# Batch 2 of a fused attention and feed-forward kernel: q before k, halved units, earlier loads

## The chip, the cores and the metric

The kernel runs on one core of a Trainium2 chip. The metric is the device time of one execution in microseconds (us). A core has TensorE for matrix products (PE in the profile, PEld for its weight loads), VectorE (DVE), ScalarE (ACT) and GpSimd (POOL) for elementwise work, and SyncE (SP), which here issues nearly all DMA transfers. Each engine works through its own queue in order, and semaphores tie the queues together.

## The reference

Eight batches of eight heads, 576 tokens and 64 features go through a linear attention whose features carry a cosine and a sine of the position. The result, 4608 tokens of 512 features, goes through a two-layer feed-forward network with a leaky ReLU.

```python
q_p = phi(q, cos_w, sin_w)      # concat(relu(q) * cos, relu(q) * sin)
k_p = phi(k, cos_w, sin_w)
kv = np.einsum('bhsf,bhsd->bhfd', k_p, v)
z = np.sum(k_p, axis=2)
num = np.einsum('bhsf,bhfd->bhsd', q_p, kv)
den = np.einsum('bhsf,bhf->bhs', q_p, z)[..., None] + 1e-06
x = num / den                   # then tokens in rows, all heads side by side
h = x @ w_in                    # 512 -> 2048
g = np.maximum(0.01 * h, h)
out = g @ w_out                 # 2048 -> 512
```

## The kernel before, in words

**Tiling.** Each batch gives a group of 512 tokens in four slices j of 128. The remaining 64 tokens of all batches make up a ninth group. Products run in float16 with float32 sums in PSUM.

**The steps of a batch.** `load_main` (L88) and `load_kvtail` (L98) bring q, k and v into staging buffers; `load_k` and `load_v` also bring the 64 tail tokens. A staging buffer is shared by tensors in turn, so a load waits until the tensor before it has been read. `q_part` and `k_part` (L337, L269) apply relu and the cosine (part 0) or sine (part 1), on VectorE or ScalarE. This is what the change's name calls rotating. `v_main` and `v_tail` (L278, L281) cast v. `q_transpose_dma` (L345) turns a slice of q with a DMA from SyncE's queue. `kv_all` (L309) makes kv on TensorE: for each half of the heads sixteen matmuls on the main tokens, and then two on the tail. ScalarE copies it out. `num` (L376) multiplies a slice of q with kv and calls `divide` (L390), three VectorE steps (den, rden, xs). Its sums lie in the PSUM pool "n", which has one buffer. kv_all and the f1 pair m = 2, 3 use that pool as well. `x_transpose` (L442) turns xs back on TensorE into the pool "o", and ScalarE copies it into xT.

**Feed-forward.** `f1_pair` (L746) makes one tile m of 128 hidden features of group 1: four matmuls of 512 tokens (L496), and after every second m an Lrelu on ScalarE into g. Later groups use a scheme of seven products of half-size blocks instead of eight. `w1_sums`, `w2_sums`, `x_sums` and `g_sums` make the sums of blocks that it needs, on VectorE. `w2_sums(i, s)` (L526) makes step s for half i of the second weight. The second layer of group 1 already uses that scheme (`f2_stream(1)`, output name ps_o, L883). Its PSUM banks are opened by `open_banks` over the pools "h", "o" and "n" of the stage before.

**What sets the order.** Up to L706 the order of the instructions is the order of the code. Among the last of these lines are the end of group 0's second layer (`ffn2`, `ffn2_out`), the divisions of batch 1 (`num_half`, L408), and the first two tiles m of each half of the first layer (`f1_half`). Behind that, all steps are put on one line with a position (`put`), sorted by position, ties in the order in which they were put, and issued so. On each engine the steps run in that order. The positions stand in tables written by hand: AT for each batch (kc and ks for k's cosine and sine, with the tail as fifth entry; v; kv; qc and qs; qt for the q transposes; num; xt; load), W2_AT for `w2_sums`, G1_AT for `g_sums` of group 1. ENG says for each k, v and q step which engine does it. Positions of batches 2 and 3 count from the start of the line. Four matmuls of `f1_pair` stand at each even position 2n (L1044), and a unit below is such a group of four. The first four tiles n are made ahead of the line, so there `f1_pair` issues only the Lrelus. For batch 2 all q parts are on VectorE, k is on VectorE but for two sine slices on ScalarE, and v is shared. For batch 3 the first q cosine part and the second sine part are on ScalarE.

Of the kernel before, what the change touches and what calls it, by code (L numbers as in the profile page):

```python
# [18 lines left out]
def kernel(  # L19
# [60 lines left out]
    ACT, DVE, POOL = nc.scalar, nc.vector, nc.gpsimd  # L80
# [152 lines left out]
    kv = [const.tile([P, H, NE], dt.float16, name=f"kv{b}") for b in range(B)]  # L233
# [20 lines left out]
    def sub(o, a, b):  # L254
        nc.vector.tensor_tensor(out=o, in0=a, in1=b, op=ALU.subtract)  # L255
# [62 lines left out]
    def kv_half(b, hg, where, blanks=0):  # L318
        ps = psum(where, [P, MAIN], dt.float32, "ps_kvh")
        idle(blanks, ps)  # L320
        ps = ps[:, 0 : 4 * NE]
        kv_mm(b, hg, ps)
        nc.scalar.copy(
            kv[b][:, 4 * hg : 4 * hg + 4, 0 : NE - 1],
            ps.rearrange("p (h e) -> p h e", h=4)[:, :, 0 : NE - 1],
        )
# [10 lines left out]
    def q_part(g, j, part, eng, lo=0, hi=H):  # L337
        src, c, _ = q_src(g, j)
        if lo == 0 and part == 0:
            st["qp", g, j] = qppool.tile([P, H, F], dt.float16, name="qp", tag="qp")  # L340
        qp, f = st["qp", g, j], part * D
        col = (cos_t, sin_t)[part][:, c : c + 1]
        phi_half(eng, qp[:, lo:hi, f : f + D], src[:, lo:hi], col)
# [126 lines left out]
    def ffn2(g, i, eng=DVE):  # L470
        tt, part = divmod(i, 4)
        if part == 0 and ("ps_o", g, tt) not in st:
            st["ps_o", g, tt] = psum("o", [P, DM], dt.float32, "ps_o")
        ps = st["ps_o", g, tt]
        for m in range(4 * part, 4 * part + 4):
            nc.tensor.matmul(
                ps,
                lhsT=st["g", g][:, m, tt * P : (tt + 1) * P],
                rhs=w2[:, m, :],
                start=(m == 0),  # L480
                stop=(m == NFT - 1),
            )
        if part == 3 and eng is not None:
            ffn2_out(g, tt, eng)

    def ffn2_out(g, tt, eng):
        osb = opool.tile([P, DM], dt.float32, name="osb", tag="osb")
        copy(eng, osb, st["ps_o", g, tt])
        nc.sync.dma_start(out_rows(g)[:, tt, :], osb)
# [4 lines left out]
    def f1_mm(g, m, ps, chunks=range(NKC), lo=0, hi=MAIN):  # L494
        for c in chunks:
            nc.tensor.matmul(  # L496
                ps[:, lo:hi],
                lhsT=w1[m // 4][c // 2][:, c % 2, m % 4 : 512 : 4],
                rhs=st["xT", g][:, c, lo:hi],
                start=(c == 0 and lo == 0),  # L500
                stop=(c == NKC - 1 and hi == MAIN),
            )
# [23 lines left out]
    def w2_sums(i, s):  # L526
        lo, hi = slice(4 * i, 4 * i + 4), slice(8 + 4 * i, 12 + 4 * i)
        left, right = slice(0, N2), slice(N2, DM)
        b11, b12 = w2[:, lo, left], w2[:, lo, right]
        b21, b22 = w2[:, hi, left], w2[:, hi, right]  # L530
        if s == 1:
            sub(wb[1][:, lo], b12, b11)
        elif s == 2:
            sub(wb[2][:, lo], b22, wb[1][:, lo])
        elif s == 4:
            sub(wb[4][:, lo], b21, wb[2][:, lo])
        else:
            sub(b12, b22, b12)
# [127 lines left out]
    ps = psum("n", [P, 2, DM], dt.float32, "ps_o")  # L666
# [22 lines left out]
    ps = psum("h", [P, 2, MAIN], dt.float16, "ps_x")  # L689
    for jp in range(2):  # L690
        x_transpose_half(1, jp, 0, ps[:, :, jp * 2 * P : (jp + 1) * 2 * P], False)
    nc.scalar.copy(st["xT", 1][:, 0:2, :], ps)
    kv_half(1, 1, "n")
    ffn2_out(0, 0, DVE)
    ffn2(0, 4 * 1 + 3, None)
    ffn2_out(0, 1, ACT)
    num_half(1, 0, 1, "h")
# [45 lines left out]
                [P, NH, N2], dt.float16, name="g" + nm, tag="g" + nm, bufs=bufs  # L743
            )

    def f1_pair(g, m):  # L746

        early_ = m % NH < 2
        if m % 2 == 0 and not early_:
            st["h", m // 2] = psum("hn"[m == 2], [P, 2, MAIN], dt.float32, "ps_h")  # L750
        ps = st["h", m // 2]
        if not early_:
            f1_mm(g, m, ps[:, m % 2])
        if m % 2:
            up, u = divmod(m - 1, NH)
            nc.scalar.activation(
                st["gt", g][:, up, :, u : u + 2].rearrange("p h m n -> p m h n"),
                ps.rearrange("p m (h n) -> p m h n", h=2),
                AF.Lrelu,
            )  # L760
# [265 lines left out]
    def put(pos, f, *args):  # L1026
        line.append((pos, len(line), f, args))
# [13 lines left out]
    put(-1, quarters, 1)  # L1041
    order = [m + up for m in range(0, NH, 2) for up in (0, 1, NH, NH + 1)]
    for n, m in enumerate(order):
        put(2 * n, f1_pair, 1, m)  # L1044
    put(31, open_banks)
    put(35, blank_seed)
    for g in range(2, NG):
# [16 lines left out]


    W1_AT = {3: (43.5, 53.5)}
    W2_AT = {2: (17.0,), 3: (30.0, 18.5), 4: (75.5,)}
    G1_AT = {3: (15.0, 31.0), 2: (17.5, 33.5), 1: (25.5, 39.5), 4: (63.0, 47.0)}
    G_AT = {3: (-6.5, 10.5), 2: (11.0, 11.0), 1: (19.5, 32.5), 4: (23.0, 29.5)}
    G3_AT = {3: (-3.5, 13.0), 2: (2.0, 23.0), 1: (12.5, 29.5), 4: (26.5, 51.0)}  # L1070
# [1 line left out]
    GL_AT = {3: (-15.5, 13.0), 2: (-1.5, 13.5), 1: (5.5, 16.2), 4: (17.5, 32.0)}  # L1072
    R_AT = (29.5, 30.0, 41.0, 48.0)
    ENG = {2: {'kc': (DVE, DVE, DVE, DVE, DVE), 'ks': (ACT, DVE, DVE, ACT, DVE), 'v': (ACT, DVE, ACT), 'qc': (DVE, DVE, DVE, DVE), 'qs': (DVE, DVE, DVE, DVE)}, 3: {'kc': (ACT, ACT, ACT, DVE, DVE), 'ks': (DVE, DVE, ACT, ACT, DVE), 'v': (DVE, ACT, DVE), 'qc': (ACT, DVE, DVE, ACT), 'qs': (DVE, ACT, ACT, DVE)}, 4: {'kc': (ACT, ACT, DVE, ACT, ACT), 'ks': (DVE, ACT, DVE, DVE, DVE), 'v': (DVE, DVE, ACT), 'qc': (DVE, DVE, ACT, DVE), 'qs': (DVE, DVE, DVE, ACT)}, 5: {'kc': (DVE, DVE, DVE, DVE, DVE), 'ks': (DVE, DVE, DVE, DVE, DVE), 'v': (DVE, ACT, ACT), 'qc': (ACT, ACT, DVE, ACT), 'qs': (ACT, ACT, DVE, ACT)}}
    AT = {2: {'kc': (-12.0, -0.5, 13.0, 5.5, 13.0), 'ks': (-22.5, -12.5, -17.0, -10.5, 0.0), 'v': (11.0, 11.0, 12.5), 'kv': (16.5,), 'qc': (-8.0, 2.5, 4.5, 8.0), 'qs': (0.0, 4.5, 7.5, 13.0), 'qt': (6.0, 7.0, 8.0, 14.0), 'num': (19.0, 20.5, 24.0, 26.5), 'xt': (24.4, 24.9, 26.9, 30.9), 'xs': (35.5, 50.0, 36.0, 56.0)}, 3: {'load': (20.0, 24.0, 29.0), 'kc': (37.0, 42.5, 47.0, 49.0, 50.5), 'ks': (34.0, 43.5, 58.5, 50.5, 51.0), 'v': (56.0, 57.5, 59.0), 'kv': (62.0,), 'qc': (26.0, 28.5, 31.0, 33.5), 'qs': (31.5, 29.5, 41.0, 41.0), 'qt': (32.5, 34.5, 44.0, 53.0), 'num': (69.5, 76.0, 83.0, 89.0), 'xt': (89.5, 92.5, 93.0, 100.5), 'xs': (102.5, 106.0, 104.5, 113.5)}, 4: {'load': (-75.5, -104.5, -111.5), 'kc': (-80.0, -58.0, -55.0, -70.5, -49.5), 'ks': (-72.5, -54.5, -66.0, -55.0, -54.0), 'v': (-85.0, -40.5, -44.5), 'kv': (-37.5,), 'qc': (-72.5, -67.5, -50.0, -40.5), 'qs': (-65.5, -51.0, -43.5, -39.0), 'qt': (-52.0, -39.5, -33.0, -32.0), 'num': (-34.0, -28.3, -24.6, -16.4), 'xt': (-19.0, -16.8, -12.1, -8.4), 'xs': (-0.5, 0.0, 9.5, 16.5)}, 5: {'load': (-103.5, -85.5, -75.5), 'kc': (-64.5, -75.0, -78.0, -50.0, -49.0), 'ks': (-71.0, -59.0, -72.5, -60.5, -74.0), 'v': (-60.0, -52.0, -60.5), 'kv': (-46.5,), 'qc': (-87.0, -76.0, -44.5, -48.0), 'qs': (-72.5, -75.5, -44.0, -31.5), 'qt': (-55.0, -53.0, -43.5, -23.5), 'num': (-37.0, -32.3, -22.6, -15.9), 'xt': (-25.0, -14.8, -17.6, -8.9), 'xs': (-2.0, -2.0, -1.5, 5.0)}}

    def loads(b, which):
        if which == 0:
# [11 lines left out]
        put(W1_AT[3][i], w1_sums, i, 3, 0, 4 - 2 * i)  # L1090
    for s, at_ in zip((1, 2, 4, 3), R_AT):
        put(top[ALL - 1] + at_, w1_sums, 1, s, 2, 4)
    for s, at_ in W2_AT.items():
        for i in range(2 - len(at_), 2):
            put(at_[i - 2], w2_sums, i, s)
    for s, at_ in G1_AT.items():
        for u in range(2):
            put(at_[u], g_sums, 1, s, 4 * u, 4 * u + 4)
# [6 lines left out]
    for b in range(2, NG):  # L1105
        at_, eng, s0 = AT[min(b, 5)], ENG[min(b, 5)], top[b] if b > 3 else 0
        if b < B:
            for n, pos_ in enumerate(at_.get("load", ())):
                put(s0 + pos_, loads, b, n)
            put(s0 + min(at_["kc"] + at_["ks"]) - 0.01, kp_tiles, b)  # L1110
            for j in range(J + 1):
                put(s0 + at_["kc"][j], k_part, b, j, 0, eng["kc"][j])
                put(s0 + at_["ks"][j], k_part, b, j, 1, eng["ks"][j])
            for n in range(3):
                put(s0 + at_["v"][n], v_part, b, n, eng["v"][n])
            put(s0 + at_["kv"][0], kv_all, b)
        else:
            for j in range(J):
                put(s0 - 100 + 3 * j, load_qtail, j)
        for j in range(J):  # L1120
            put(s0 + at_["qc"][j], q_part, b, j, 0, eng["qc"][j])
            put(s0 + at_["qs"][j], q_part, b, j, 1, eng["qs"][j])
            put(s0 + at_["qt"][j], q_transpose_dma, b, j)
            put(s0 + at_["num"][j], num, b, j)
            put(s0 + at_["xt"][j], x_transpose if b == 2 else x_transpose_dma, b, j)
            put(s0 + at_["xs"][j], x_sums, b, j + 1)
# [33 lines left out]
```

## Time and profile before

| what | us |
|---|---|
| median of 3 runs | 271.92 |
| the runs | 271.84, 275.43, 271.92 |
| the profiled execution, its own time | 271.19 |
| its span, first to last instruction | 269.4 |

The page of the profile gives each engine's busy time and share of the span. Timelines list instructions in order of time, runs of like ones merged: start, duration, engine, line, operation, output and inputs, count, and in brackets the idle time before it and what ended it. The view of stretches gives the length and then for PE, PEld, DVE, ACT and POOL the busy time and the count, then the granted clock of TensorE, the DMA share and GB/s. The chain of waits lists start, duration and what was running. A DMA issue is listed with its size and the time to landing.

### The profile page before, as it was taken

How to read it: one execution, taken by the hardware profiler on the slowest of the kernel's cores; microseconds unless marked ns; L12 is line 12 of the kernel's file. 1: busy time of each engine (PE TensorE's matmuls, PEld its weight loads, DVE VectorE, ACT ScalarE, POOL GpSimd, SP SyncE). 2: the span in 40 equal slices, each digit the busy share in tenths (PEclk: the TensorE clock that was granted, in tenths of full speed). 3: DMA queues.
4: the chain of work that ended last, by engine and by line, in shares of the span. 5: the costliest groups of instructions: out<-in, count | busy, mean ns of one | idle time of the engine just before them, and what ended most of it. 6: DMA issues, size and time to landing. Idle time of an engine off the chain costs nothing.

```text
span 269.4 us, 6623 instructions
## 1 busy us (share of the span) xinstructions
PE 263.5 (98%) x2670; PEld 227.0 (84%) x2670; DVE 203.8 (76%) x452; ACT 199.4 (74%) x329; POOL 13.1 (5%) x25
## 2 busy tenths in 40 slices
PE   8999999999999999999999999999999999999994
PEld 6985455665998989899999999999999899999983
DVE  5875798797967898888879778977687758545652
ACT  8757476696888896978888788878877757666720
POOL 5047001000000000000000000000000000000000
PEclk9999999999999999999999999999999999999999
DMA  6999999979999979958995899669384412200324
GB/s 226 373 392 415 393 386 373 357 170 296 274 252 313 191 195 249 354 116 285 259 254 122 271 239 247 156 202 154 62 142 155 61 41 97 80 0 2 156 41 117
DMA packets 86190, 57.05 MB, mean 212 GB/s; under 512 B 55632, under 2 KB 81232, under 8 KB 85648
## 3 DMA queue, kind: packets, MB, share of 16 engines
q1 hardware_dynamic: 85584, 55.98, 77.0%
q8 instruction: 21, 0.34, 0.6%
q10 hardware_dynamic: 448, 0.39, 0.4%
q0 software_dynamic: 128, 0.26, 0.3%
q14 instruction: 9, 0.07, 0.1%
HBM read 36.70 MB, written 9.44 MB: 171 GB/s over the span
## 4 chain that ended last, share of the span: by engine, by line
PE 76%; DVE 2%; issue 0%
PE ps_o L883 33%; PE ps_h L782 30%; PE ps_h L496 4%; PE ps_num L381 3%; PE ps_h L883 3%; PE ps_kv L290 2%; DVE gs L255 0%; PE ps_kv L299 0%; PE ps_xt L446 0%; DVE xs L397 0%; DVE w L255 0%; DVE wb L255 0%; DVE ob L252 0%; DVE qp L241 0%; DVE kpt L241 0%
## 5 line engine op out<-in xcount | busy, mean ns | idle before, releaser
L883 PEld LDWEIGHTS <-g 128*128 128x128 f16 x648 | 62.7, 98 | 7.2 <-DVE g L252 0.3
L252 DVE TENSOR_TENSOR u<-ps_h,u 128x512 f32<-128x512 f32 x52 | 35.8, 688 | 21.0 <-PE ps_h L782 19.3
L883 PE MATMUL ps_o<-w,g 128*128 128x256 f16 x352 | 51.2, 273 | 0.0
L782 PEld LDWEIGHTS <-w 128*128 128x128 f16 x416 | 44.7, 113 | 1.2
L782 PE MATMUL ps_h<-xT,w 128*128 128x256 f16 x288 | 43.3, 273 | 0.0
L809 ACT ACTIVATE g<-u 128x1024 f16<-128x1024 f32 x26 | 27.5, 1058 | 11.2 <-DVE u L252 10.9
L802 ACT COPY u<-ps_h 128x512 f32<-128x512 f32 x52 | 30.5, 586 | 7.1 <-PE ps_h L782 7.0
L795 ACT ACTIVATE g<-ps_h 128x512 f16<-128x512 f32 x52 | 31.2, 602 | 5.6 <-PE ps_h L782 5.6
L782 PEld LDWEIGHTS <-wa 128*128 128x128 f16 x312 | 33.7, 113 | 1.2
L883 PE MATMUL ps_o<-wb,g 128*128 128x256 f16 x232 | 33.5, 273 | 0.0
L782 PE MATMUL ps_h<-xw,wa 128*128 128x256 f16 x208 | 31.3, 273 | 0.0
L883 PEld LDWEIGHTS <-gs 128*128 128x128 f16 x256 | 24.9, 98 | 2.9
L901 ACT COPY ob<-ps_o 128x512 f32<-128x512 f32 (+1 forms) x32 | 18.1, 565 | 11.9 <-PE ps_o L883 10.6
L496 PE MATMUL ps_h<-xT,w 128*128 128x512 f16 (+1 forms) x104 | 24.7, 363 | 0.0
L397 DVE TENSOR_TENSOR xs<-ps_num,rden 128x512 f16<-128x512 f32 x28 | 19.4, 691 | 1.0
L883 PE MATMUL ps_o<-w,gs 128*128 128x256 f16 x120 | 17.8, 273 | 0.0
L252 DVE TENSOR_TENSOR ob<-ps_o,ob 128x512 f32<-128x512 f32 (+1 forms) x22 | 14.9, 675 | 3.8 <-ACT ob L901 1.9
L883 PE MATMUL ps_o<-wb,gs 128*128 128x256 f16 x120 | 17.5, 273 | 0.0
L792 ACT COPY ps_h<-ps_h 128x512 f32<-128x512 f32 x26 | 14.9, 572 | 2.4 <-PE ps_h L782 1.5
L255 DVE TENSOR_TENSOR gs<-g 128x1024 f16<-128x1024 f16 x16 | 11.0, 688 | 7.3 <-ACT g L809 7.2
L782 PE MATMUL ps_h<-xw,w 128*128 128x256 f16 x104 | 15.6, 273 | 0.0
L782 PE MATMUL ps_h<-xT,wa 128*128 128x256 f16 x104 | 15.6, 273 | 0.0
(116 smaller groups left out, 411.8 us busy)
## 6 DMA issues: line engine op xcount, KB each, us to landing
qst<-in_q_dram SPq DMA_DIRECT2D x7, 1024.0 KB, 6.4
out_dram<-ob SPq DMA_DIRECT2D x14, 512.0 KB, 2.8
kst<-in_k_dram SPq DMA_DIRECT2D x6, 1024.0 KB, 7.1
vst<-in_v_dram SPq DMA_DIRECT2D x6, 1024.0 KB, 7.2
w1st<-in_moe_w_in_dram SPq DMA_DIRECT2D x8, 512.0 KB, 10.5
w2st<-in_moe_w_out_dram SPq DMA_DIRECT2D x4, 1024.0 KB, 12.3
kst<-in_k_dram SPq DMA_DIRECT2D x4, 512.0 KB, 8.1
vst<-in_v_dram SPq DMA_DIRECT2D x4, 512.0 KB, 8.3
```

The costliest lines, as they stand in the source:

```text
L252: nc.vector.tensor_tensor(out=o, in0=a, in1=b, op=ALU.add)
L255: nc.vector.tensor_tensor(out=o, in0=a, in1=b, op=ALU.subtract)
L381: nc.tensor.matmul(ps[lo:hi, h // 4, (h % 4) * NE : (h % 4 + 1) * NE - 1], lhsT=qpT[:, h, lo:hi], rhs=kv[b][:, h, 0 : NE - 1],)
L397: nc.vector.tensor_tensor(out=xs, in0=ps[:, :, 0 : 4 * NE].rearrange("p a (b e) -> p a b e", e=NE)[:, :, :, 0:D], in1=rden.rearrange("p (a ...
L496: nc.tensor.matmul(ps[:, lo:hi], lhsT=w1[m // 4][c // 2][:, c % 2, m % 4 : 512 : 4], rhs=st["xT", g][:, c, lo:hi], start=(c == 0 and lo == 0),
L782: nc.tensor.matmul(bank[:, p], lhsT=w(c), rhs=st["xb", g][n][:, c], start=(fresh and p == 0 and c == 0), stop=(c == 1), skip_group_check=True,
L792: nc.scalar.copy(bank1[bj], bank1[bi])
L795: nc.scalar.activation(st["g" + nm, g][:, 2 * t : 2 * t + 2], bank1[bi], AF.Lrelu)
L802: nc.scalar.copy(st["u", g, t][:, n], bank1[bi])
L809: nc.scalar.activation(st["gt", g][:, :, 1, 2 * t : 2 * t + 2], st["u", g, t], AF.Lrelu)
L883: nc.tensor.matmul(bank[..., lo:hi], lhsT=st[G2[n], g][:, m, pair * P : (pair + 1) * P], rhs=W2[n](m)[:, lo:hi], start=(fresh and m == 0), ...
L901: nc.scalar.copy(o_at(g, half_, col, pair), bank_of(bi, pair, pair is None))
```

## The change

The change leaves every computation as it is and moves steps.

- `w2_sums(1, 2)` leaves position 17 and comes ahead of the last `ffn2_out` on VectorE in group 0. Both q parts of slice 0 of batch 2 come right behind that `ffn2_out`, ahead of batch 1's last two divisions.
- `f1_pair` is cut in two parts of two matmuls, at positions 2n and 2n + 1. The Lrelu stands at the second part.
- Batch 2's other q parts and all its q transposes go to the front of the line, ahead of most k parts. Of k, only the two sine slices on ScalarE and the sine of slice 1 stay at negative positions.
- Batch 3's loads of q, k and v move from 20, 24 and 29 to -14, 15 and 16. In SyncE's queue they stay behind batch 2's q transposes.
- num of batch 2 moves from 19, 20.5, 24, 26.5 to 19.2, 22.2, 25.2, 28.2. Its x transposes move from 24.4, 24.9, 26.9, 30.9 to 24.0, 27.2, 30.2, 30.9. kv stays at 16.5, and v at 11, 11 and 12.5.
- `w2_sums(1, 3)` moves from 18.5 to 17.4.

```diff
     nc.scalar.copy(st["xT", 1][:, 0:2, :], ps)
     kv_half(1, 1, "n")
+    w2_sums(1, 2)
     ffn2_out(0, 0, DVE)
+    for part in range(2):
+        q_part(2, 0, part, DVE)
     ffn2(0, 4 * 1 + 3, None)
...
-    def f1_pair(g, m):
+    def f1_pair(g, m, part):
...
-        if m % 2 == 0 and not early_:
+        if m % 2 == 0 and part == 0 and not early_:
             st["h", m // 2] = psum("hn"[m == 2], [P, 2, MAIN], dt.float32, "ps_h")
         ps = st["h", m // 2]
         if not early_:
-            f1_mm(g, m, ps[:, m % 2])
-        if m % 2:
+            f1_mm(g, m, ps[:, m % 2], (2 * part, 2 * part + 1))
+        if m % 2 and part:
...
-        put(2 * n, f1_pair, 1, m)
+        for part in range(2):
+            put(2 * n + part, f1_pair, 1, m, part)
...
-    W2_AT = {2: (17.0,), 3: (30.0, 18.5), 4: (75.5,)}
+    W2_AT = {(0, 3): 30.0, (1, 3): 17.4, (1, 4): 75.5}
...
-    AT = {2: {'kc': (-12.0, -0.5, 13.0, 5.5, 13.0), 'ks': (-22.5, -12.5, -17.0, -10.5, 0.0),
-         'qc': (-8.0, 2.5, 4.5, 8.0), 'qs': (0.0, 4.5, 7.5, 13.0), 'qt': (6.0, 7.0, 8.0, 14.0),
-         'num': (19.0, 20.5, 24.0, 26.5), 'xt': (24.4, 24.9, 26.9, 30.9)},
-         3: {'load': (20.0, 24.0, 29.0)}}
+    AT = {2: {'kc': (2.5, 4.5, 7.5, 8.0, 13.0), 'ks': (-22.5, -12.5, 0.0, -10.5, 4.5),
+         'qc': (None, -22.0, -19.0, -16.0), 'qs': (None, -21.0, -18.0, -15.0), 'qt': (-22.5, -20.5, -17.5, -14.5),
+         'num': (19.2, 22.2, 25.2, 28.2), 'xt': (24.0, 27.2, 30.2, 30.9)},
+         3: {'load': (-14.0, 15.0, 16.0)}}
...
-            put(s0 + at_["qc"][j], q_part, b, j, 0, eng["qc"][j])
-            put(s0 + at_["qs"][j], q_part, b, j, 1, eng["qs"][j])
+            for part, nm in enumerate(("qc", "qs")):
+                if at_[nm][j] is not None:
+                    put(s0 + at_[nm][j], q_part, b, j, part, eng[nm][j])
```

The two tables are shown with their changed entries alone.

More of the change, by code (lines that the diff above doesn't have):

```diff
@@ L1074 @@
     ENG = {2: {'kc': (DVE, DVE, DVE, DVE, DVE), 'ks': (ACT, DVE, DVE, ACT, DVE), 'v': (ACT, DVE, ACT), 'qc': (DVE, DVE, DVE, DVE), 'qs': (DVE, DVE, DVE, DVE)}, 3: {'kc': (ACT, ACT, ACT, DVE, DVE), 'ks': (DVE, DVE, ACT, ACT, DVE), 'v': (DVE, ACT, DVE), 'qc': (ACT, DVE, DVE, ACT), 'qs': (DVE, ACT, ACT, DVE)}, 4: {'kc': (ACT, ACT, DVE, ACT, ACT), 'ks': (DVE, ACT, DVE, DVE, DVE), 'v': (DVE, DVE, ACT), 'qc': (DVE, DVE, ACT, DVE), 'qs': (DVE, DVE, DVE, ACT)}, 5: {'kc': (DVE, DVE, DVE, DVE, DVE), 'ks': (DVE, DVE, DVE, DVE, DVE), 'v': (DVE, ACT, ACT), 'qc': (ACT, ACT, DVE, ACT), 'qs': (ACT, ACT, DVE, ACT)}}
-    AT = {2: {'kc': (-12.0, -0.5, 13.0, 5.5, 13.0), 'ks': (-22.5, -12.5, -17.0, -10.5, 0.0), 'v': (11.0, 11.0, 12.5), 'kv': (16.5,), 'qc': (-8.0, 2.5, 4.5, 8.0), 'qs': (0.0, 4.5, 7.5, 13.0), 'qt': (6.0, 7.0, 8.0, 14.0), 'num': (19.0, 20.5, 24.0, 26.5), 'xt': (24.4, 24.9, 26.9, 30.9), 'xs': (35.5, 50.0, 36.0, 56.0)}, 3: {'load': (20.0, 24.0, 29.0), 'kc': (37.0, 42.5, 47.0, 49.0, 50.5), 'ks': (34.0, 43.5, 58.5, 50.5, 51.0), 'v': (56.0, 57.5, 59.0), 'kv': (62.0,), 'qc': (26.0, 28.5, 31.0, 33.5), 'qs': (31.5, 29.5, 41.0, 41.0), 'qt': (32.5, 34.5, 44.0, 53.0), 'num': (69.5, 76.0, 83.0, 89.0), 'xt': (89.5, 92.5, 93.0, 100.5), 'xs': (102.5, 106.0, 104.5, 113.5)}, 4: {'load': (-75.5, -104.5, -111.5), 'kc': (-80.0, -58.0, -55.0, -70.5, -49.5), 'ks': (-72.5, -54.5, -66.0, -55.0, -54.0), 'v': (-85.0, -40.5, -44.5), 'kv': (-37.5,), 'qc': (-72.5, -67.5, -50.0, -40.5), 'qs': (-65.5, -51.0, -43.5, -39.0), 'qt': (-52.0, -39.5, -33.0, -32.0), 'num': (-34.0, -28.3, -24.6, -16.4), 'xt': (-19.0, -16.8, -12.1, -8.4), 'xs': (-0.5, 0.0, 9.5, 16.5)}, 5: {'load': (-103.5, -85.5, -75.5), 'kc': (-64.5, -75.0, -78.0, -50.0, -49.0), 'ks': (-71.0, -59.0, -72.5, -60.5, -74.0), 'v': (-60.0, -52.0, -60.5), 'kv': (-46.5,), 'qc': (-87.0, -76.0, -44.5, -48.0), 'qs': (-72.5, -75.5, -44.0, -31.5), 'qt': (-55.0, -53.0, -43.5, -23.5), 'num': (-37.0, -32.3, -22.6, -15.9), 'xt': (-25.0, -14.8, -17.6, -8.9), 'xs': (-2.0, -2.0, -1.5, 5.0)}}
@@ new lines @@
+    AT = {2: {'kc': (2.5, 4.5, 7.5, 8.0, 13.0), 'ks': (-22.5, -12.5, 0.0, -10.5, 4.5), 'v': (11.0, 11.0, 12.5), 'kv': (16.5,), 'qc': (None, -22.0, -19.0, -16.0), 'qs': (None, -21.0, -18.0, -15.0), 'qt': (-22.5, -20.5, -17.5, -14.5), 'num': (19.2, 22.2, 25.2, 28.2), 'xt': (24.0, 27.2, 30.2, 30.9), 'xs': (35.5, 50.0, 36.0, 56.0)}, 3: {'load': (-14.0, 15.0, 16.0), 'kc': (37.0, 42.5, 47.0, 49.0, 50.5), 'ks': (34.0, 43.5, 58.5, 50.5, 51.0), 'v': (56.0, 57.5, 59.0), 'kv': (62.0,), 'qc': (26.0, 28.5, 31.0, 33.5), 'qs': (31.5, 29.5, 41.0, 41.0), 'qt': (32.5, 34.5, 44.0, 53.0), 'num': (69.5, 76.0, 83.0, 89.0), 'xt': (89.5, 92.5, 93.0, 100.5), 'xs': (102.5, 106.0, 104.5, 113.5)}, 4: {'load': (-75.5, -104.5, -111.5), 'kc': (-80.0, -58.0, -55.0, -70.5, -49.5), 'ks': (-72.5, -54.5, -66.0, -55.0, -54.0), 'v': (-85.0, -40.5, -44.5), 'kv': (-37.5,), 'qc': (-72.5, -67.5, -50.0, -40.5), 'qs': (-65.5, -51.0, -43.5, -39.0), 'qt': (-52.0, -39.5, -33.0, -32.0), 'num': (-34.0, -28.3, -24.6, -16.4), 'xt': (-19.0, -16.8, -12.1, -8.4), 'xs': (-0.5, 0.0, 9.5, 16.5)}, 5: {'load': (-103.5, -85.5, -75.5), 'kc': (-64.5, -75.0, -78.0, -50.0, -49.0), 'ks': (-71.0, -59.0, -72.5, -60.5, -74.0), 'v': (-60.0, -52.0, -60.5), 'kv': (-46.5,), 'qc': (-87.0, -76.0, -44.5, -48.0), 'qs': (-72.5, -75.5, -44.0, -31.5), 'qt': (-55.0, -53.0, -43.5, -23.5), 'num': (-37.0, -32.3, -22.6, -15.9), 'xt': (-25.0, -14.8, -17.6, -8.9), 'xs': (-2.0, -2.0, -1.5, 5.0)}}
@@ L1092 @@
         put(top[ALL - 1] + at_, w1_sums, 1, s, 2, 4)
-    for s, at_ in W2_AT.items():
-        for i in range(2 - len(at_), 2):
-            put(at_[i - 2], w2_sums, i, s)
+    for (i, s), at_ in W2_AT.items():
+        put(at_, w2_sums, i, s)
     for s, at_ in G1_AT.items():
```

## The prediction

> **What bounds the kernel now.** I read the page's first lines, then busy time by stretches, then TensorE's own timeline around batch 2, then the chain of waits for the price of each matmul.
>
> ```profile
> span 269.4 us, 6623 instructions
> PE 263.5 (98%) x2670; PEld 227.0 (84%) x2670; DVE 203.8 (76%) x452; ACT 199.4 (74%) x329; POOL 13.1 (5%) x25
> ```
> ```profile
> 60.00:64.00 4.00, 3.54 (x37) 2.06 (x35) 2.37 (x9) 1.86 (x2) 0.00 (x0) 1.00 0.86 226
> ...
> 68.00:208.00 140.00, 140.00 (x1489) 129.80 (x1488) 115.81 (x250) 117.20 (x198) 0.00 (x0) 1.00 0.93 215
> ```
> ```profile
> 57.50 0.67 PE L290 MATMUL ps_kv<-vmain,kpm 128*128 128x65 f16 x16
> 58.01 0.28 PE L299 MATMUL ps_kv<-vtail,kpt 128*128 128x130 f16 x2
> ...
> 58.75 1.02 PE L496 MATMUL ps_h<-xT,w 128*128 128x512 f16 x4
> 59.61 0.42 PE L381 MATMUL ps_num<-kv,qpT 128*128 128x65 f16 x8
> 59.87 1.03 PE L496 MATMUL ps_h<-xT,w 128*128 128x512 f16 x4
> 61.36 0.41 PE L381 MATMUL ps_num<-kv,qpT 128*128 128x65 f16 x8 [0.46 <-DVE xs L397]
> ...
> 64.04 1.03 PE L496 MATMUL ps_h<-xT,w 128*128 128x512 f16 x4
> 65.07 0.41 PE L381 MATMUL ps_num<-kv,qpT 128*128 128x65 f16 x8
> ...
> 65.55 1.89 PE L496 MATMUL ps_h<-xT,w 128*128 128x512 f16 x8
> ...
> 67.50 0.71 PE L883 MATMUL ps_o<-w,g 128*128 128x256 f16 x5
> ```
> ```profile
> 63.50 0.26 PE ps_num L381 x8
> ...
> 65.71 1.73 PE ps_h L496 x8
> 67.44 0.22 PE ps_xt L446 x4
> 67.66 1.31 PE ps_o L883 x12
> ```
>
> TensorE bounds it: 98% busy, and wholly busy from 68 to 208 us. So only holes in TensorE's own stream are worth anything. Matmul ends are modelled, so I take prices from the chain: a 512-wide matmul 1.73/8 = 0.216 us, four of them 0.86 (one unit), eight num matmuls 0.26, four transposes 0.22. In the timeline, four unit matmuls from 59.87 end at 60.73; the second num starts at 61.36: a hole of 0.62 us (the row says 0.46 by modelled ends). From 64.04, 64.90; the fourth num starts at 65.07: 0.17. That is 0.79 us of holes at batch 2, and nothing else after 52 us that this change touches. Even if both close, the gain is 0.79 of 271, or 0.3%.
>
> **The change part by part.** The total of TensorE work stays. I walk it from the first unit that changes place to the start of the second stage's ps_o matmuls, 67.50 us before.
>
> *Work put into VectorE's gaps.*
>
> ```profile
> 46.68 0.69 DVE L249 COPY osb<-ps_o 128x512 f32<-128x512 f32 x1 [0.68 <-PE ps_o L476]
> 48.93 0.17 DVE L392 TENSOR_SCALAR den<-ps_numh 128x8 f32<-128x8 f32 x1 [1.55 <-PE ps_numh L417]
> ...
> 51.01 0.88 DVE L241 TENSOR_SCALAR kpm<-kst,sin_t 128x512 f16<-128x512 f32 x2
> ...
> 58.88 0.69 DVE L255 TENSOR_TENSOR gs<-g,gs 128x1024 f16<-128x1024 f16 x1
> 59.49 0.68 DVE L255 TENSOR_TENSOR w<-w 128x1024 f16<-128x1024 f16 x1
> 60.09 0.16 DVE L392 TENSOR_SCALAR den<-ps_num 128x8 f32<-128x8 f32 x1
> ```
> ```profile
> qst<-in_q_dram SPq DMA_DIRECT2D x1, 1024.0 KB, 11.2
> ```
>
> w2_sums(1, 2) takes 0.60 (58.88 to 59.49) and goes into the 0.68 gap before the osb copy. The two q parts of batch 2, slice 0 take 0.40 each (0.88 for two that overlap by 0.08) and go into the 1.55 gap ahead of the division at 48.93. Their q was issued at 35.84 and lands 11.2 later, at 47.04, before 47.37 when the copy ends. Cost nothing; if q came over 0.7 late, the division and TensorE's transposes behind it would be late by the rest. What it saves: VectorE's back-to-back run from 51.01 gets 1.4 us shorter. But that run delayed the first division hardly: num starts at 59.61, and 0.45 later (the lag of the second, 61.36 to 61.81, below), at 60.06, its sums are there; the division began at 60.09. Worth 0.03.
>
> *q ahead of k.* After 51.01 VectorE does six q parts (2.4 us, to 53.4), then seven 0.40 k parts, one 0.27 tail part, the 0.60 v cast and the last tail part: the last k part ends near 57.0 (57.37 before). Work for kv is no later. The four q transposes then wait only for SyncE.
>
> *kv half a unit earlier.* f1_pair is cut into halves at 2n and 2n+1, so kv at 16.5 comes behind 2, not 4, matmuls of its unit. TensorE reaches it 0.43 earlier, at 57.07. ScalarE's steps keep their order:
>
> ```profile
> 53.36 2.84 ACT L756 ACTIVATE g<-ps_h 128x1024 f16<-128x1024 f32 x3
> 56.07 1.06 ACT L247 CAST vmain<-vst 128x1024 f16<-128x1024 f32 x1
> 57.00 0.93 ACT L222 ACTIVATE vtail<-vtl,odd 128x256 f16<-128x256 f32 x2
> ...
> 58.95 0.59 ACT L313 CAST kv<-ps_kv 128x520 f16<-128x520 f32 x1
> ```
>
> ScalarE is full here, and nothing the change moves stands ahead of these. vmain ends at 57.13, vtail at 57.93. Before, the vtail matmuls came at 58.01, just in time. Now kv starts at 57.20 (a wait of 0.13), its 16 matmuls take 0.51, and the vtail matmuls wait from 57.71 to 58.00 (0.29). kv ends at 58.75, as before, with 0.42 us of new hole; matmuls behind it stand in the same queue. Below: 0, if ScalarE ran 0.8 earlier; above: 0.43, the whole half unit. I take 0.42, as all its rows are known.
>
> *nums 1.5 units apart.*
>
> ```profile
> 61.81 0.17 DVE L392 TENSOR_SCALAR den<-ps_num 128x8 f32<-128x8 f32 x1 [0.60 <-PE ps_num L381]
> ...
> 62.25 0.69 DVE L397 TENSOR_TENSOR xs<-ps_num,rden 128x512 f16<-128x512 f32 x1
> ```
>
> One PSUM buffer serves all nums, so the next starts a round trip later: 61.36 to 62.94 is 1.58, plus 0.15 to wake TensorE (first product's end 60.52 + 0.69 = 61.21, to 61.36), 1.73. Behind kv stand 6 matmuls (1.30), so num 0 starts at 60.05 (59.61 before). Six matmuls stand between nums: TensorE is at num 1 at 60.05 + 0.26 + 1.30 = 61.61, allowed at 61.78: hole 0.17. num 2 has a transpose group between too: 0.26 + 1.30 + 0.22 = 1.78, no hole (63.56); num 3 likewise (65.34). Behind it four matmuls and the third transposes (66.68), then the fourth, which need num 3's division: 65.34 + 1.58 + 0.08 = 67.00. Hole 0.32 (0.25 to 0.40 by a wake of 0.01 to 0.15), where before 8 matmuls hid it. With 0.22 and the last half unit (0.43) ps_o starts at 67.65.
>
> *Loads.*
>
> ```profile
> 49.44 2.19 SPq L489 DMA_DIRECT2D out_dram<-osb  x4
> 53.80 5.95 SPq L347 DMA_TRANSPOSE qpT<-qp  x4
> 59.84 0.54 SPq L93 DMA_DIRECT2D qst<-in_q_dram  x1
> ```
> ```profile
> qst<-in_q_dram SPq DMA_DIRECT2D x1, 1024.0 KB, 6.2
> ```
>
> SyncE's queue is in order: v's load, the stores to 51.63, then the transposes, then q of batch 3. The transposes now find their q ready when SyncE is free, at 51.7, and q of batch 3 follows as far behind as before (59.84 - 53.80 = 6.04): issued at 57.74, landing 6.2 later at 63.94. k and v follow, all 2.1 us earlier than before. ScalarE first reads this q at 64.1: Lrelu behind num 1's half unit, 0.42 later than its matmuls as before, then the first xT copy. Cost nothing; v of batch 2 is still landing at 51.7, so the transposes may take longer, which is rival 2's opening. num 0 needs its transpose only at 60.05. W2_AT's 18.5 to 17.4 only swaps two VectorE steps ahead of num 0: nothing.
>
> *Sum.* Holes 0.42 + 0.17 + 0.32 = 0.91 in place of 0.79; ps_o starts 0.15 later (67.65 against 67.50; the 0.03 between is rounding and I keep 0.15). From there TensorE is wholly busy, VectorE's first wait on it (an add behind ps_o) comes within 4 us, so all shifts alike. The profiled execution of 271.19 (span 269.4 and 1.8 around it) becomes 271.34; the median of the runs shown, 271.92, is 0.73 above that execution, so 272.07.
>
> *A page against a row.* With the 0.62 hole inside it, the stretch 60 to 64 still shows a granted clock of 1.00. The Trainium skill, "TensorE: Matmul & The Clock Gate", section "A second HAM failure mode: psum-queue depth-cycling", says that frequent micro-idles between groups of matmuls can make the clock swing between half and full. By the row the sum stays 272.07; by the page the four short holes could cost a spell at half clock, the fourth case below; so far the trace goes against it here.
>
> **The rivals.**
>
> *1. It does what it says.* If ScalarE's casts are through 0.8 earlier than my order gives, kv doesn't wait: num 0 at 59.62, ps_o at 67.22, 0.28 sooner than before: 271.6. If division trips are shorter too, all 0.79 go: 271.1. For: VectorE is 1.4 lighter. Against: the ScalarE rows, which hold nothing that left.
>
> *2. q of batch 3 late on ScalarE: slower.*
>
> ```profile
> 65.11 1.02 ACT L756 ACTIVATE g<-ps_h 128x1024 f16<-128x1024 f32 x1
> 66.13 0.72 ACT L239 ACTIVATE qp<-qst,cos_t 128x512 f16<-128x512 f32 x1
> 66.76 0.57 ACT L447 COPY xT<-ps_xt 128x512 f16<-128x512 f16 x1
> ```
> ```profile
> kst<-in_k_dram SPq DMA_DIRECT2D x1, 1024.0 KB, 12.2
> ```
>
> The q part at 26.0 now stands ahead of the Lrelu at 27, two xT copies and another q part, where before it stood behind that Lrelu. ps_o's first bank is free only when the third xT copy is: two q parts of 0.62 (66.13 to 66.76 with its overlap), an Lrelu of 0.95 (2.84 / 3), copies of 0.49 and 0.57, and 0.05 to wake: about 3.3 us after q lands. It decides from a landing at 64.35 on (67.65 less 3.3), only 0.4 after my 63.94; each tenth beyond costs a tenth. With a landing of 12.2 (k of batch 2) instead of 6.2 it is 69.94, ps_o at 73.24, 5.6 later: 277.7. Against: the link is less crowded after 57 than when k came.
>
> *3. Clock.*
>
> ```profile
> 1.09 5.33 PE L168 MATMUL ps_idle<-blank 128*128 128x256 f16 x28 [1.09 <-DVE blank L162]
> ```
>
> 28 matmuls of 256 took (5.33 - 0.27)/28 = 0.18 each at the start, against 1.31/12 = 0.109 later. One such spell costs 28 x 0.07 = 2 us: 274.1. Against: the clock of 1.00 at a longer hole.
>
> **How the numbers follow.** Forecast 0.50 (own range 271.9 to 272.3); rival 1 0.31; rival 2 0.16, most of it under 1 us and 0.03 past 2%; rival 3 0.03. A difference under 2%, 5.4 us, can't be told from no change in this kernel's runs. Faster by that would need more hole than there is: 0.01, for a row misread. Slower 0.03; within 0.96. The range runs from rival 1's far end, 271.0, to 273.0, a q that lands 0.9 beyond 64.35.
>
> **What would show it.** Right: kv near 57.2 with its vtail matmuls waiting on ScalarE until 58.0; num 0 at 60.05; nums 1.75 apart; the fourth transposes waiting on VectorE's xs; q of batch 3 issued near 57.7; ps_o near 67.65. Wrong: kv starts at 57.07 without a wait, or ScalarE waits for qst near 64 us, or the granted clock falls between 57 and 70.

## The result, and the profile after

The changed kernel takes 272.8 us (median of 22 runs), the kernel before 271.8 (22 runs). The ratio is 1.004, with a 95% interval of 1.0027 to 1.0053: about 1.1 us slower, well under 2%. The forecast was 0.15 us slower. Its four holes are in the trace almost to the hundredth, but the loss came by its second rival: batch 3's q was late for ScalarE.

First, TensorE's timeline after the change, around batch 2 (start, duration, line, output and inputs, count).

```profile
51.22 0.40 PE L434 MATMUL ps_xth<-ident,xp 128*128 128x128 f16 x4
...
58.28 0.67 PE L290 MATMUL ps_kv<-vmain,kpm 128*128 128x65 f16 x16
59.09 0.28 PE L299 MATMUL ps_kv<-vtail,kpt 128*128 128x130 f16 x2
...
61.12 0.42 PE L381 MATMUL ps_num<-kv,qpT 128*128 128x65 f16 x8
...
62.85 0.41 PE L381 MATMUL ps_num<-kv,qpT 128*128 128x65 f16 x8
...
64.62 0.42 PE L381 MATMUL ps_num<-kv,qpT 128*128 128x65 f16 x8
...
66.40 0.42 PE L381 MATMUL ps_num<-kv,qpT 128*128 128x65 f16 x8
...
67.53 0.92 PE L446 MATMUL ps_xt<-ident,xs 128*128 128x128 f16 x8
68.28 0.59 PE L496 MATMUL ps_h<-xT,w 128*128 128x512 f16 x2
69.06 1.47 PE L886 MATMUL ps_o<-w,g 128*128 128x256 f16 x12 [0.19 <-ACT xT L447]
```

The two holes at batch 2, 0.62 and 0.17, have become five. By the starts of single matmuls, less the prediction's prices (0.216 us for 512 columns, other widths in proportion), they are 0.12 before kv, 0.30 before its tail matmuls, 0.18 before num 1, 0.30 inside the last transposes, and 0.35 before ps_o. The last was not in the sum. The chain of waits shows where it comes from (start, duration, what ran):

```profile
...
65.50 0.31 issue
65.81 0.39 ACT qp L239
66.19 0.24 issue
66.44 1.00 ACT g L759
67.44 0.48 ACT xT L447
67.91 0.62 ACT qp L239
68.53 0.49 ACT xT L447
69.02 0.04 issue
69.06 1.47 PE ps_o L886 x12
```

From 65.81 to 69.06 the chain is on ScalarE: batch 3's q part, an Lrelu, the second xT copy, another q part, the third xT copy. ps_o's first bank is free only behind that copy. SyncE's queue shows why that q part starts at 65.81:

```profile
49.20 2.17 SPq L489 DMA_DIRECT2D out_dram<-osb  x4
51.47 7.67 SPq L347 DMA_TRANSPOSE qpT<-qp  x4
59.20 0.58 SPq L93 DMA_DIRECT2D qst<-in_q_dram  x1
```
```profile
qst<-in_q_dram SPq DMA_DIRECT2D x1, 1024.0 KB, 6.5
```

The transposes start 2.3 us earlier than before and take 7.67 us instead of 5.95, so q is issued at 59.20, only 0.6 earlier, and lands 6.5 later, at 65.70.

Two profiles compare badly by their absolute times. The stretch that the change touches begins with the x transposes of batch 1's last halves (L434). It starts at 51.22 here and at 50.11 in the profile before, and it started between 50.13 and 51.02 in the eleven others below, whatever the kernel. The difference between these two profiles arises early, at the first batch's work: TensorE is 1.1 us behind from 16 us on. So below I give the stretch from the first L434 transposes to the first ps_o matmul, 17.38 before and 17.85 after. Behind it, from the first ps_o matmul to the last matmul of the kernel, all these profiles have 197.81 to 197.94. One profiled execution, that of e3 below, ran at a granted clock of 0.559 and took 460 us, so its trace is not read.

### The profile page after: what moved, and what is told of

Read it like the earlier page. It is cut to its first block, busy times and chain, and to the rows that moved or that the text cites. A ratio compares the mean times of both kernels' runs of the same rounds, so it can differ in the third digit from the quotient of the medians.

```text
span 271.1 us, 6625 instructions
## 1 busy us (share of the span) xinstructions
PE 264.3 (97%) x2670; PEld 227.2 (84%) x2670; DVE 204.0 (75%) x452; ACT 199.5 (74%) x329; POOL 13.1 (5%) x25
## 4 chain that ended last, share of the span: by engine, by line
PE 89%; DMA 4%; ACT 3%; SPq 1%; DVE 1%; issue 1%; POOL 0%
PE ps_o L886 33%; PE ps_h L785 30%; PE ps_h L460 5%; PE ps_o L476 5%; PE ps_h L496 5%; DMA vst<-in_v_dram 4%; PE ps_h L886 3%; PE ps_num L381 3%; PE ps_kv L290 2%; ACT g L759 1%; SPq L93 1%; PE ps_qt L366 1%; PE ps_kv L299 1%; PE ps_numh L417 1%; PE ps_kvh L290 1%
## 5 line engine op out<-in xcount | busy, mean ns | idle before, releaser
L886 PEld LDWEIGHTS <-gs 128*128 128x128 f16 x256 | 24.9, 98 | 2.9
L496 PE MATMUL ps_h<-xT,w 128*128 128x512 f16 (+1 forms) x104 | 25.2, 363 | 0.0
L886 PE MATMUL ps_o<-w,gs 128*128 128x256 f16 x120 | 17.8, 273 | 0.0
L886 PE MATMUL ps_o<-wb,gs 128*128 128x256 f16 x120 | 17.5, 273 | 0.0
```

Source lines behind the costliest of these rows:

```text
L496: nc.tensor.matmul(ps[:, lo:hi], lhsT=w1[m // 4][c // 2][:, c % 2, m % 4 : 512 : 4], rhs=st["xT", g][:, c, lo:hi], start=(c == 0 and lo == 0),
L886: nc.tensor.matmul(bank[..., lo:hi], lhsT=st[G2[n], g][:, m, pair * P : (pair + 1) * P], rhs=W2[n](m)[:, lo:hi], start=(fresh and m == 0), ...
```

## The experiments

**Theories.** A: the loss is made by kv's hold and the spacing of the nums, and holes add up. C: batch 3's q, through ScalarE's order, sets when ps_o starts, whatever lies ahead. B: the change also costs time ahead of the stretch.

| kernel | stretch starts | q part starts on ScalarE | ps_o starts | stretch | ratio to before, 95% |
|---|---|---|---|---|---|
| before | 50.11 | 66.13 | 67.50 | 17.38 | |
| e0, before again | 50.31 | 66.65 | 67.90 | 17.58 | |
| after | 51.22 | 65.81 | 69.06 | 17.85 | 1.0027 to 1.0053 |
| e1, loads back | 50.45 | 65.93 | 69.19 | 18.73 | 1.0008 to 1.0037 |
| e2, kv back | 50.13 | 66.02 | 69.28 | 19.15 | 1.0011 to 1.0052 |
| e3b, q parts later | 50.89 | 67.01 | 68.39 | 17.49 | 0.9983 to 1.0006 |
| e6, q load ahead | 50.20 | 64.10 | 67.69 | 17.49 | 0.9987 to 1.0021 |
| e8, gaps only | 50.20 | 66.10 | 67.58 | 17.38 | 0.9986 to 1.0009 |
| e9, ScalarE swap only | 50.97 | 66.38 | 68.53 | 17.56 | 1.0011 to 1.0033 |
| e5 | 50.62 | 68.81 | 67.58 | 16.97 | 0.9970 to 1.0007 |
| e7 | 50.38 | 68.52 | 67.16 | 16.78 | 0.9979 to 1.0020 |
| e7b, e7 again | 50.40 | 68.55 | 67.18 | 16.78 | 0.9978 to 1.0006 |
| e10 | 51.02 | 69.16 | 67.80 | 16.78 | 0.9966 to 0.9989 |

**e0: the kernel before, another execution.**

> The kernel before, a second look. The stretch from the first x transposes of batch 1's last halves (L434, the second-last group before the first layer's long run) to the first ps_o matmul was 17.39 us before (50.11 to 67.50) and 17.84 us after (51.22 to 69.06). Theory A, the loss is made inside this stretch: 17.4 again within 0.1, while the time ahead of the stretch differs from look to look (50.11 and 51.22 in the two profiles, by waits on the first loads). Theory B, the change also costs time ahead of the stretch: the stretch starts at 50.1 again within 0.2, and near 51.2 in every run of the changed kernel.

It started at 50.31, and the kernels of the changed order started at 50.13 and 50.45 in e2 and e1. That is against B: a kernel of the changed order can reach the stretch as early as the kernel before. The stretch was 17.58 with a hole of 0.2 before ps_o that the first profile doesn't have. Theory A's 17.4 within 0.1 missed it. ScalarE's timeline of e0:

```profile
65.31 1.02 ACT L756 ACTIVATE g<-ps_h 128x1024 f16<-128x1024 f32 x1
66.65 0.72 ACT L239 ACTIVATE qp<-qst,cos_t 128x512 f16<-128x512 f32 x1 [0.31 <-DMA qst<-in_q_dram]
67.28 0.57 ACT L447 COPY xT<-ps_xt 128x512 f16<-128x512 f16 x1
```

Even in the order before, q came late here, and the third xT copy, 0.6 behind the q part, ended at 67.85, just ahead of ps_o at 67.90. So the kernel before already stood at the edge of this wait.

**e1: batch 3's loads back.**

```diff
-'load': (-14.0, 15.0, 16.0)
+'load': (20.0, 24.0, 29.0)
```

> The changed kernel with batch 3's loads back at positions 20, 24 and 29. SyncE's queue has nothing else between those places and the new ones, so its order stays. Theory A (the loads' move does nothing): the stretch is 17.84 within 0.15, with the same holes, and the time is that of the changed kernel, ratio 1.002 to 1.006. Rival (the earlier loads crowd the link and make the transposes and q late): the stretch falls by the 0.35 hole ahead of ps_o to 17.5 and q parts of batch 3 on ScalarE wait no more.

The stretch was 18.73, so both numbers for it missed. What it tells is in its absolute times: q was issued at 59.60, the q part began at 65.93, and ps_o at 69.19, 3.26 behind it. The execution reached the stretch 0.77 sooner than the profile after, and ps_o came no sooner. The positions of the loads do nothing, as SyncE's queue has nothing between the old place and the new: in both traces every engine runs the same list of instructions. So e1 is in effect the changed kernel once more, and 17.85 against 18.73 is how far two executions of one order lie apart in this stretch.

**e2: kv back by half a unit.**

```diff
-'kv': (16.5,)
+'kv': (17.5,)
```

> The changed kernel with kv at 17.5, behind both halves of its unit, as before the change. Theory A (holes add up): the 0.42 us in which kv waited for ScalarE's casts goes, num 0 starts 0.42 sooner, the stretch falls from 17.84 to 17.4 and the ratio to before by 0.0015. Rival C (the end of the stretch is set by q of batch 3 landing, then ScalarE's q part, Lrelu and copies, 3.3 us): the holes ahead close but the one before ps_o grows from 0.35 to 0.77, and the stretch stays at 17.8.

TensorE's timeline:

```profile
66.04 0.39 PE L446 MATMUL ps_xt<-ident,xs 128*128 128x128 f16 x4
68.18 0.38 PE L446 MATMUL ps_xt<-ident,xs 128*128 128x128 f16 x4 [1.76 <-ACT xT L447]
68.40 0.59 PE L496 MATMUL ps_h<-xT,w 128*128 128x512 f16 x2
69.28 0.92 PE L886 MATMUL ps_o<-w,g 128*128 128x256 f16 x7 [0.28 <-ACT xT L447]
```

kv's two holes are gone and num 0 starts at 59.63, yet ps_o starts at 69.28, 3.26 behind the q part. All that was won ahead, and the earlier start of this execution, stands at the fourth transposes as a hole of 1.92 (from 66.26, where the third transposes are through by their price, to 68.18) and before ps_o. The ratio, 1.0032, is no nearer to 1 than e1's 1.0022. This fits C and not A: the holes ahead don't add up, the wait for q swallows them. C's stretch of 17.8 missed because it took the landing to move with the start; it doesn't: q landed at 65.98 here and at 65.70 in the profile after, which started 1.09 later.

**e3 and e3b: batch 3's q parts later on ScalarE.**

```diff
-'qc': (26.0, 28.5, 31.0, 33.5), 'qs': (31.5, 29.5, 41.0, 41.0)
+'qc': (27.3, 28.5, 31.0, 33.5), 'qs': (31.5, 31.1, 41.0, 41.0)
```

> The changed kernel with batch 3's two q parts on ScalarE moved behind the work that frees PSUM: the cosine part from 26.0 to 27.3 (behind the Lrelu and the second xT copy), the sine part from 29.5 to 31.1. Theory A and rival C agree: the hole of 0.35 ahead of ps_o goes, the stretch falls to 17.5, and the third xT copy starts when its transposes are done. If the bank's copy isn't what ps_o waited for, the hole stays.

Its ratio was 0.9996 (0.9971 to 1.0022). The same kernel ran again for its trace:

> The changed kernel with batch 3's first two ScalarE q parts moved from 26.0 to 27.3 and from 29.5 to 31.1, so that fewer PSUM-freeing steps stand behind them. In three profiles of the changed order the first ps_o matmul came 3.25 to 3.26 us after the start of that q part (65.81 to 69.06, 65.93 to 69.19, 66.02 to 69.28), whatever the holes ahead. Theory C (that q part sets the start of ps_o): ps_o then comes about 17.5 after the L434 transposes (the holes of 0.42, 0.18 and 0.30 stay, the ones at the fourth transposes and ahead of ps_o fall to 0.30 and nothing) and the time falls to within 0.2 us of before. Theory A (kv's hold and the spacing of the nums make the loss): ps_o stays at 69 and the ratio at 1.003 to 1.004.

The stretch was 17.49 and the ratio 0.9995 (0.9983 to 1.0006). The hole before ps_o is gone, the other four are as they were (0.12, 0.30, 0.18, 0.30). ScalarE's timeline, and TensorE's:

```profile
65.62 1.02 ACT L759 ACTIVATE g<-ps_h 128x1024 f16<-128x1024 f32 x1 [0.71 <-PE ps_h L496]
66.55 0.58 ACT L447 COPY xT<-ps_xt 128x512 f16<-128x512 f16 x1
67.01 0.73 ACT L239 ACTIVATE qp<-qst,cos_t 128x512 f16<-128x512 f32 x1
67.64 1.10 ACT L447 COPY xT<-ps_xt 128x512 f16<-128x512 f16 x2
```
```profile
67.95 0.59 PE L496 MATMUL ps_h<-xT,w 128*128 128x512 f16 x2
68.39 0.82 PE L886 MATMUL ps_o<-w,g 128*128 128x256 f16 x6
```

The places of two q parts on ScalarE are thus worth the whole measured loss, as far as the intervals tell.

**e9: that order alone, in the kernel before.**

```diff
-'qc': (26.0, 28.5, 31.0, 33.5)
+'qc': (25.9, 28.5, 31.0, 33.5)
```

> The kernel before with one ScalarE swap and nothing else: batch 3's first q cosine part at 25.9 instead of 26.0, so ahead of the Lrelu of its unit as in the changed kernel. Theory C: that q part starts when q lands, near 66.0 to 66.6, behind it come an Lrelu (0.92) and the third xT copy (0.57), so ps_o starts 2.2 after the q part's start, at 68.2 to 68.8, 0.7 later than before, ratio 1.002 to 1.003. Theory A (kv and the spacing of the nums make the loss, the order on ScalarE doesn't matter): ps_o at 67.5 to 67.9, ratio 1.000.

ScalarE's timeline, and the first ps_o of TensorE's:

```profile
66.38 0.72 ACT L239 ACTIVATE qp<-qst,cos_t 128x512 f16<-128x512 f32 x1 [0.43 <-DVE g L252]
67.00 1.00 ACT L756 ACTIVATE g<-ps_h 128x1024 f16<-128x1024 f32 x1
67.91 0.58 ACT L447 COPY xT<-ps_xt 128x512 f16<-128x512 f16 x1
```
```profile
68.53 0.71 PE L883 MATMUL ps_o<-w,g 128*128 128x256 f16 x5
```

ps_o starts 2.16 behind the q part, at 68.53; in e0, where the q part waited for q as well but stood behind the Lrelu, it was 1.25. The ratio is 1.0022 (1.0011 to 1.0033), with every other engine's order untouched. So swapping one Lrelu with one q part makes the kernel slower by itself, by 0.6 us. That is about half of what the change costs: in the changed kernel the second xT copy and the other q part stand between as well, and ps_o comes 3.25 behind. The profile of e9 alone doesn't show it, as its hole before ps_o, 0.18, is no longer than the 0.2 of e0. The idle time ahead of the q part is put down by the trace to a VectorE step that ends at the same moment. But q was issued at 60.47 and landed 5.8 later, at 66.27, and the q part started 0.1 behind that, as it did in e0 (66.54, 66.65) and after the change (65.70, 65.81); the landing is the better reading.

**e6: q of batch 3 issued two transposes sooner.**

```diff
-'qt': (-22.5, -20.5, -17.5, -14.5)
+'qt': (-22.5, -20.5, -13.9, -13.8)
```

> The changed kernel with batch 3's q load issued between the second and the third q transposes of batch 2 instead of behind the fourth (SyncE's order changes only there). Theory C: q is issued near 55.6 instead of 59.3 and lands 3 us sooner, the q part on ScalarE doesn't hold the Lrelu any more, ps_o comes 17.5 after the L434 transposes, and the time is within 0.2 us of before. Rival: the load's packets make the third and fourth transposes late, num 2 or num 3 waits for them, and the stretch stays at 17.8 or more.

SyncE's timeline:

```profile
51.70 3.90 SPq L347 DMA_TRANSPOSE qpT<-qp  x2
55.70 0.54 SPq L93 DMA_DIRECT2D qst<-in_q_dram  x1
56.33 5.57 SPq L347 DMA_TRANSPOSE qpT<-qp  x2
```

q is issued at 55.70, the q part starts at 64.10 behind its own predecessors, and the stretch is 17.49 with the same four holes. The two transposes behind the load take 5.57 to issue, but num 2 and num 3 still come 1.78 apart and don't wait. The ratio, 1.0004 (0.9987 to 1.0021), can't be told from before. So the wait goes either by moving the reader or by moving the load.

**e8: only the work put into VectorE's gaps.** The kernel before, with `w2_sums(1, 2)` and batch 2's first two q parts at the changed places.

```diff
     kv_half(1, 1, "n")
+    w2_sums(1, 2)
     ffn2_out(0, 0, DVE)
+    for part in range(2):
+        q_part(2, 0, part, DVE)
...
-    W2_AT = {2: (17.0,), 3: (30.0, 18.5), 4: (75.5,)}
+    W2_AT = {3: (30.0, 18.5), 4: (75.5,)}
...
```

> The kernel before with one part of the change alone: w2_sums(1, 2) and batch 2's first two q parts in VectorE's gaps at batch 1's last divisions. The prediction has this at nothing (VectorE's run ahead of num 0 is 1.4 us shorter, but num 0's division began only 0.03 late): the holes of 0.62 and 0.17 stay, the stretch is 17.4 to 17.6, ratio 0.9995 to 1.0005. Rival: VectorE bound the stretch, and it falls by up to 0.6.

17.38 with holes of 0.63 and 0.17, ratio 0.9998 (0.9986 to 1.0009): nothing, as forecast.

**e5, e7, e10: closing the holes.** e5 puts the changed kernel's kv at 17.5, its ScalarE q parts behind the last xT copy, and the fourth transposes behind the last half unit. e7 also moves the third transposes. e10 also moves batch 3's third ScalarE q part. Only the changed entries are shown, put side by side.

```diff
-'kv': (16.5,), 'xt': (24.0, 27.2, 30.2, 30.9), put(31, open_banks)
+'kv': (17.5,), 'xt': (24.0, 27.2, 30.2, 31.2), put(31.5, open_banks)   # e5
+'kv': (17.5,), 'xt': (24.0, 27.2, 29.2, 31.2), put(31.5, open_banks)   # e7, e10
...
-'qc': (26.0, 28.5, 31.0, 33.5), 'qs': (31.5, 29.5, 41.0, 41.0)
+'qc': (31.3, 28.5, 31.0, 33.5), 'qs': (31.5, 31.4, 41.0, 41.0)         # e5, e7
+'qc': (31.3, 28.5, 31.0, 37.0), 'qs': (31.5, 31.4, 41.0, 41.0)         # e10
```

> The changed kernel with kv at 17.5, both q parts of batch 3 behind the last xT copy (31.3, 31.4), and the fourth x transposes behind the last half unit (31.2, the banks opened at 31.5). Theory C with the holes as sized: of 0.79 before only the 0.18 at num 1 is left, the L434 transposes to ps_o take 16.8, and the ratio to before is 0.9975 to 0.9985. If the order of q against k, or the halves themselves, cost something more, it stays at 17.4 or above.

The stretch was 16.97, between the two numbers: 0.18 stayed at num 1, and 0.19 stood before ps_o, where the third xT copy now came right ahead of it. The ratio, 0.9988 (0.9970 to 1.0007), is not clear of 1.

> The changed kernel with kv at 17.5, the fourth x transposes at 31.2, both ScalarE q parts behind the last xT copy, and in addition the third x transposes at 29.2 instead of 30.2, since in the run without that ps_o waited 0.19 for the copy of the third transposes. Theory: only the 0.18 at num 1 is left, the L434 transposes to ps_o take 16.8 (17.38 before), and everything behind takes 197.81 as in every profile: 0.6 less, ratio 0.9975 to 0.9985. If something else holds ps_o, the stretch stays at 16.97.

16.78 as expected, with a new hole of 0.13 behind the first ps_o matmuls. The ratio, 1.0 (0.9979 to 1.0020), leaves the time open.

> The same kernel as e7_best, timed again, since one run of 274.27 widened its interval to 0.998 to 1.002. Theory: the L434 transposes to ps_o take 16.78 again and a hole of 0.13 stands behind the first ps_o matmuls, where ScalarE's copy of that bank waits behind three q parts of batch 3; 0.47 less than before in all, ratio 0.998 to 0.999. Rival: the holes closed here open elsewhere, ratio 1.000.

The same holes, 0.9992 (0.9978 to 1.0006): still not clear.

> e7_best with batch 3's third ScalarE q part moved from 33.5 to 37.0, behind the copy of the first ps_o bank. The hole of 0.13 behind the first ps_o matmuls goes, all else stays: the stretch 16.78, behind it 197.81 (197.94 in e7_best), ratio 0.9975 to 0.9985.

TensorE's timeline of e10:

```profile
60.51 0.42 PE L381 MATMUL ps_num<-kv,qpT 128*128 128x65 f16 x8
60.77 1.46 PE L496 MATMUL ps_h<-xT,w 128*128 128x512 f16 x6
62.25 0.41 PE L381 MATMUL ps_num<-kv,qpT 128*128 128x65 f16 x8
...
67.57 0.39 PE L446 MATMUL ps_xt<-ident,xs 128*128 128x128 f16 x4
67.80 1.47 PE L886 MATMUL ps_o<-w,g 128*128 128x256 f16 x12
```

Only the 0.18 at num 1 is left. Stretch 16.78, behind it 197.82, ratio 0.9977 (0.9966 to 0.9989), median 271.1: faster than both kernels, by about 0.6 us against before. Of the four runs that close holes (e5, e7, e7b, e10), this is the only one whose interval lies wholly below 1. The idea of nums 1.5 units apart holds once kv, the last transposes and ScalarE's order fit it.

## Why the prediction was right or wrong, point by point

**VectorE's gaps, at nothing: right.** After the change the sums run from 47.02, the copy from 47.78, the q parts from 48.39, and the division at 50.03 still waits for TensorE. e8 shows the part alone at 0.9998.

**q ahead of k, no later for kv: right.** The last k part ends at 58.07, which is 56.96 in the time of the profile before (less 1.11); the forecast was near 57.0.

**kv half a unit early, 0.42: right.** 0.12 and 0.30.

**Nums and fourth transposes, 0.17 and 0.32: right.** 0.18 and 0.30, and the nums came 1.73, 1.77 and 1.78 apart. The four holes make 0.90 against 0.91.

**The loads, at nothing: the step that failed.** The prediction had q follow "as far behind as before (59.84 - 53.80 = 6.04): issued at 57.74, landing 6.2 later at 63.94". It took the transposes to need the same time wherever they start. Started at 51.47 instead of 53.80, they took 7.67, as the second and third took 2.16 and 2.23 instead of 1.24 and 1.25. So q was issued 7.73 behind the first of them, at 59.20, and landed at 65.70.

By rival 2's own condition, a landing from 64.35 on, ScalarE's new order then sets ps_o; TensorE is 1.11 later in this profile, so the point lies at 65.46 there. The rival's "about 3.3 us" measured 3.25. ScalarE waiting for qst, one of the prediction's own signs of being wrong, came: not near 64, but until 65.81. The prediction named the opening (transposes that take longer) and gave the rival 0.16; it is what happened in every profile with the changed ScalarE order and q behind the transposes (after, e1, e2). One more thing stood in the lines it showed: before the change, q landed at 66.04 (59.84 + 6.2), 0.1 ahead of its first reader at 66.13, so there was hardly any slack to spend.

**The sum: right holes, wrong rule.** Holes ahead of a wait that ends at a fixed time don't add up. ps_o started at 69.06, 69.19 and 69.28 with holes of 0.60, 0.60 and 0.18 ahead of the fourth transposes, and in stretches that started 1.1 us apart. The three profiles of the order before with this wait absent or small (before, e0, e8) had 67.50, 67.90 and 67.58. On average the first three are 1.5 later, against 1.0 in the medians; profiles are single executions, and how the rest divides was not tried. The forecast of 272.1 was 0.7 short of the 272.8 measured, inside its range of 271.0 to 273.0, and that is partly luck: the upper end stood for a q that lands 0.9 beyond the critical point. In e1 and e2, whose stretches start nearly as early as that of the profile before, q landed 1.2 and 1.6 beyond it (65.9 against 64.69, and 65.98 against 64.37).

**Rival 1 (it does what it says)** didn't happen: kv waited for ScalarE's casts in the changed kernel. A gain of its size came in e10, in another way, with kv moved back. **Rival 3 (the clock)** didn't happen. In the profile after, with five short holes within 11 us, the granted clock is 1.00 in every stretch from 49 to 72 us, and e2's hole of 1.92 left it at 1.00 in the stretch it lies in and the next (last four columns: POOL, clock, DMA share, GB/s). The rule of the Trainium skill that the prediction weighed, "TensorE: Matmul & The Clock Gate", section "A second HAM failure mode: psum-queue depth-cycling", speaks of frequent micro-idles between groups of matmuls. No run here shows such a swing of the clock; with so few holes, the runs don't say how frequent they would have to be.

```profile
64.00:68.00 4.00, 2.42 (x24) 1.52 (x23) 3.66 (x8) 1.98 (x3) 0.00 (x0) 1.00 1.11 372
68.00:72.00 4.00, 3.53 (x31) 2.87 (x31) 2.50 (x6) 3.81 (x8) 0.00 (x0) 1.00 1.32 303
```

## What to carry to other kernels

When a step is cut into parts, its closing instruction moves to the last part's place; look on every engine at what it now stands behind, because half a position can put a PSUM-freeing step behind a load. Before adding up holes on the bounding engine, look for one wait downstream that ends at a time of its own: it swallows savings and losses ahead of it alike. A load that is asked for earlier by position but keeps its place in its queue isn't earlier, and when what stands ahead of it is slowed, neither is what follows.

## What the runs showed of the hardware that was not expected

Issuing the same DMA transpose takes SyncE from 1.2 to 2.8 us, and what decides it stays open. Before the change the four took 1.90, 1.24, 1.25 and 1.25 us. After it they took 1.72, 2.16, 2.23 and 1.25, and landing of the first took 6.6 us instead of 3.1. With q's load ahead of the last two, as in e6, these took 5.57 together. For the first two, v and the stores may be the reason: they were issued at 51.47 and 53.30, v's last load landed near 53.0 and the last store near 55.6. The third, issued at 55.56, took longest, though nearly all packets then are of the transposes' kind (of 640 between 55 and 56 us, 631 are under 512 bytes; before the change, with transposes alone from 57 to 58, all are). The DMA share doesn't tell the slow ones from the quick one either: it was 1.21 at the third and 1.18 at the fourth. No run took the stores or v away.

```profile
53.20:55.50 2.30, 2.30 (x18) 1.76 (x16) 2.30 (x7) 2.30 (x5) 0.00 (x0) 1.00 1.23 191
55.50:57.80 2.30, 2.30 (x13) 1.19 (x11) 2.30 (x7) 2.30 (x3) 0.00 (x0) 1.00 1.21 123
57.80:59.20 1.40, 1.26 (x21) 0.83 (x20) 1.40 (x4) 1.40 (x4) 0.00 (x0) 1.00 1.18 265
```
